# Constants of the last convolution chunk loaded ahead, and its last twelve frequencies multiplied on chip

## The chip, the cores and the metric

The kernel runs on one core of one Trainium2 chip. The metric is the device time of one execution in microseconds (us). The core has a matrix engine (TensorE, PE in the profile), a vector engine (VectorE, DVE), an engine for activation functions (ScalarE, ACT), a general one (GpSimd, POOL) and one that mainly issues transfers (SyncE, SP). Each has its own queue of instructions, and DMA transfers are issued from the queues of SP, ACT and POOL. Matmul results land in PSUM, which has eight banks; everything else on chip lives in SBUF. Between them and the memory outside (DRAM) only DMA moves data.

## The reference

The reference is a block with adaptive layer norm, a long convolution and a gated MLP, on 2048 positions of 640 channels, all in float32.

```python
mod = (_silu(c) @ w_mod).reshape(c.shape[0], 6, 1, -1)
sa, ca, ga, sb, cb, gb = (mod[:, 0], mod[:, 1], mod[:, 2], mod[:, 3], mod[:, 4], mod[:, 5])
h = _layernorm(x, axis=-1) * (1 + ca) + sa
x = x + ga * _A_ref(h, ...)     # y = causal convolution of h with K, over 2048 positions, plus h * Dskip
h = _layernorm(x, axis=-1) * (1 + cb) + sb
x = x + gb * _B_ref(h, B_w1, B_w3, B_w2)     # (silu(h w1) * (h w3)) w2, with 1728 inner columns
```

K is the real part of a sum of 128 complex exponentials for each channel. The reference applies it by FFT.

## The kernel before, in words

The kernel does the convolution by a Fourier transform written as matmuls. A position is a pair of 32 (`NA`) by 64 (`NB`), a frequency a pair of 32 `f` and 64. The 640 channels go in five **chunks** of 128 (`ch` 0 to 4), each chunk in eight **groups** (`g` 0 to 7) of four `f`. A group is numbered `k = 10 + 8 * ch + g`, so the last chunk has the numbers 42 to 49.

A group passes these stages. `stage2` (tile p of the trace) multiplies the transformed input and kernel, both in `uk`, by the constants `s2`, 256 KB a group. `k_copy` (kc) takes the kernel half out of PSUM on ACT. `products` (T and p) and `sums` (Y) form the complex products on DVE. `inverse1` (pz) multiplies them by the constants `i1`, again 256 KB a group. `z_store` copies the result to `zt` on ACT and stores it to the DRAM tensor `zs`. `s2` and `i1` are loaded anew for each group of each chunk, on SP's queue, into two buffers each, so that a load must wait for the group two before it.

The rest of the inverse transform sums over `f`: 16 tiles `j` of 128 positions read `zs` back with frequency on the partitions (`z_load`) and multiply it by `i2`. For the first four tiles that happens early: `x_part(j)` takes the first four chunks (tile py), adds `x` (xw, giving xm) and takes batch-norm statistics. Two places in PSUM, tagged pk and pb, hold py.

`ROUND` is an order written out by hand, run ten times. It makes the tables of the kernel K (phases `ph` on POOL, exponentials on ACT, products on DVE, `kgen` on PE) for later steps and runs the groups behind them. The loop over `tk` after it (line 981) finishes the groups of the last chunk. There the instructions are ordered by a planner with a cost model; `issue_after` puts an instruction behind another in a queue, and `keep_in_program_order` pins it.

The last chunk's end is written out in `z_last` (line 769). Each group is stored by itself, from ACT's queue. After group 5, POOL issues eight reads for `f` 0 to 23 of the four early tiles; after group 7, SP and ACT issue four each for `f` 24 to 31. `x_first` (line 1050) then runs ten matmuls on zeros that keep PE going, the 16 matmuls with `i2` on the last chunk (written to one bank `pl`, in the trace ps<-A,i), 18 more on zeros, and takes the second layer norm's statistics: three instructions for each tile on DVE, two small ones on POOL, one on DVE. The normalized rows (tile T) are transposed on PE, and the gated products begin (`plain`, then `seven` with fewer products, and `outputs`).

The first weights and the `x` tiles 4 and 5 are loaded on SP behind the last `i1` load (lines 1001 to 1009). `x_get` loads the `z` of the later tiles; the four places of `z_tile` are first held by the early tiles.

Phase tiles come from pool `tp` with three places (line 587), each 128 partitions by 32 x 67 words.

Of the kernel before, what the change touches and what calls it, by code (L numbers as in the profile page):

```python
# [33 lines left out]
NG = NA // 8  # L34
NPG = NPH + NG - 1
TURN = 4294967296.0
EPS = 1e-5


def consts():  # L40
# [6 lines left out]
    for q in range(4):  # L47
# [40 lines left out]
    f = lambda v: np.ascontiguousarray(v, dtype=np.float32)  # L88
    return {"s1": f(s1), "s2": f(s2), "i1": f(i1), "i2": f(i2), "iota": iota, "misc": f(misc),
            "ident": np.eye(P, dtype=np.float32)}  # L90
# [25 lines left out]
def tile_kernel(ctx: ExitStack, tc: tile.TileContext, a):  # L116
# [468 lines left out]
    def phases(s):  # L585
        sl = slice(s * SD, s * SD + 2 * SD)
        p = tp.tile([P, 2 * SD, NPG], I32, name="ph", bufs=3)
# [100 lines left out]
    def inverse1_load(g):  # L688
# [3 lines left out]
        return i1  # L692

    def stage2(ch, g):
        s2 = ahead.pop((ch, g, "s2"), None)
# [56 lines left out]

    zsv = zs.rearrange("k b c f d -> (c f) b k d")
    zsw = zs.rearrange("k b c f d -> k (b c) f d")

# [13 lines left out]
    def z_last(g):  # L769

        zt = fp.tile([P, 8, DC], F32, name="zt", bufs=2)[:, :4]
        acopy(zt.rearrange("p (i r) d -> p r i d", r=2), Zq[NDC - 1][:, :, (g % 2) * 2:(g % 2) * 2 + 2, :])
        S.dma_start(zsw[NDC - 1, :, g * 4:g * 4 + 4], zt)
        if g in (5, 7):
            fs = (0, 24) if g == 5 else (24, 32)
            for j in range(4):
                for c in range(2):
                    r = slice(c * 32 + fs[0], c * 32 + fs[1])
                    ins = (nc.gpsimd if g == 5 else S if c else nc.sync).dma_start(
                        early[j][1][64 + r.start:64 + r.stop, :, 2 * DC:], zsv[r, 4 * j:4 * j + 4, NDC - 1])  # L780
                    if g == 5 or c == 0:
                        zlast[g == 5] = ins


    def z_load(z, j, ks, q=nc.sync, b0=0):

        nb = z.shape[1]
        for k in ks:
            hh = int(k > 1)
            kk = k - 2 * hh  # L790
            q.dma_start(z[hh * 64:hh * 64 + 64, :, kk * DC:kk * DC + DC],
                        zsv[:, 4 * j + b0:4 * j + b0 + nb, k])

# [20 lines left out]

    early = []
    xe = []
# [146 lines left out]
    for rnd in range(NS // EB):  # L963
        if 2 <= rnd < 7:
            late_load(rnd - 2)
        for word in ROUND:
            name, k = word[:2].rstrip("+-"), EB * rnd + int(word[len(word[:2].rstrip("+-")):])
            if name in pieces:
                if 2 <= rnd < 7:
                    pieces[name](rnd - 2)  # L970
                continue
            do(name, k)
            if name == "E1" and 30 <= k < 38 and k % 2 == 0:
                x_load((k - 30) // 2)

            if name == "kg" and 36 <= k < 40:
                early.append((None, z_tile()))
                z_load(early[-1][1], k - 36, range(3), q=nc.gpsimd)
    in_order[0] = False

    for tk in range(NS + 1, LAG + 8 * NDC + 2):
        do("st", tk)
        do("kc", tk)
        last = do("iv", tk - 1)
        do("zt", tk - 1)
        do("T", tk)
        do("Y", tk)
        if tk == NS + 1:
# [4 lines left out]
            for j in range(4):  # L993
                early[j] = (x_tile(), early[j][1], xp.tile([P, KD, 6], F32, name="st5", bufs=4))
        i = tk - 1 - LAG - 8 * NDC + 8
        if 0 <= i < 8:
            if i < 4:
                z_load(early[i][1], i, (3,), q=nc.gpsimd)
# [31 lines left out]

    IDLE = (10, 18)

# [17 lines left out]
    def x_first(tiles):  # L1050

        keep_warm(IDLE[0])
        pl = bank(0).rearrange("p (i c) -> p i c", i=4)
        mv = xp.tile([P, 4, 2], F32, name="mv4", bufs=1)
        rs = xp.tile([P, 3, 4], F32, name="rs4", bufs=1)
        for j, (x, z, st) in enumerate(early):
            for b in range(4):
                c = slice(b * NA, b * NA + NA)
                tc.keep_in_program_order(PE.matmul(pl[c, j, :], i2[64:], z[64:, b, 2 * DC:], start=True, stop=True,
                                                   tile_position=(64, c.start)))  # L1060
        keep_warm(IDLE[1])
        for j, (x, z, st) in enumerate(early):
            V.tensor_tensor(x[:, 512:], pl[:, j, :], x[:, 512:], op=OP.add)
            V.bn_stats(st[:, 4, :], x[:, 512:])
            V.bn_aggr(mv[:, j, :], st)
        e = lambda i: epst[:, i:i + 1].broadcast_to([P, 4])
        G.tensor_tensor(rs[:, 0, :], mv[:, :, 1], e(0), op=OP.add)
        power = G.tensor_tensor(rs[:, 1, :], rs[:, 0, :], e(1), op=OP.pow)
        V.scalar_tensor_tensor(rs[:, 2, :], mv[:, :, 0], -1.0, rs[:, 1, :], op0=OP.mult, op1=OP.mult)
        for j, (x, z, st) in enumerate(early):  # L1070
# [5 lines left out]
            tiles.append(xn)  # L1076
        return power

# [380 lines left out]
    for pair in range(2):  # L1459
# [13 lines left out]
        if pair == 0:  # L1473
            tiles = []
            power = x_first(tiles)
            for k in range(KD):
# [120 lines left out]
```

## Time and profile before

| | us |
|---|---|
| median of 3 runs (lowest, highest) | 943.76 (942.69, 943.88) |
| the profiled execution | 944.3 |
| its span in the trace | 942.3 |
| PE busy | 874.9 |
| DVE busy | 699.1 |
| ACT busy | 541.6 |
| POOL busy | 268.4 |

The mean clock granted to PE is 0.963 of full speed. The profile shows one execution; the span runs from the first instruction to the last, and the execution's own time has 2.0 us more around it. All times in the text are us from the span's start.

In the trace, buffer numbers are left out of tile names, so `s` stands for `s2` and also for other tiles named s, and `i` for `i1` and `i2`. `L110` is a helper through which most instructions are recorded, so groups are told apart by their tiles. An entry in square brackets gives the time that an engine was idle just before an instruction and what ended it. A name like SPq or ACTq is an engine's queue, issuing a DMA.

### The profile page before, as it was taken

Reading aid. Unit: us, or ns where it says so; the run is one execution under the profiler, and the core shown is the slowest. Engines: PE = TensorE matmul, PEld = TensorE weight load, DVE = VectorE, ACT = ScalarE, POOL = GpSimd, SP = SyncE. Lnnn points to the kernel's source line nnn. Section 1 sums busy time; section 2 is a strip of 40 time slices with the busy share of each in tenths; the row PEclk is TensorE's granted clock in tenths of the full one; section 3 lists DMA queues with packets and bytes.
Section 4 is the critical chain, followed back from the end, with each engine's and each line's share of the span. In section 5 each row is a group of like instructions: output and inputs, shape, how many; then the busy total and the mean of one; then the engine's idle time right before and its main releaser. Section 6 shows DMA issues by size and latency. Waiting matters only on the chain.

```text
span 942.3 us, 19918 instructions
## 1 busy us (share of the span) xinstructions
PE 874.9 (93%) x7950; PEld 665.5 (71%) x7950; DVE 699.1 (74%) x1209; ACT 541.6 (57%) x747; POOL 268.4 (28%) x277
## 2 busy tenths in 40 slices
PE   3788989999988888999999999999999999999997
PEld 2445566666666655678888886678888888888885
DVE  5899899999999857686666655677876666664674
ACT  6989889999999432474333322465643333323332
POOL 3333544554444011223222201320332222200341
PEclk9777689999999999999999999999999999999999
DMA  9664476576666786952111227946312322123352
GB/s 273 208 221 177 150 204 211 175 214 192 180 201 179 206 254 201 274 191 85 56 57 56 56 71 204 268 143 197 117 51 57 112 56 57 56 85 97 102 199 77
DMA packets 103279, 140.66 MB, mean 149 GB/s; under 512 B 20276, under 2 KB 62388, under 8 KB 103188
## 3 DMA queue, kind: packets, MB, share of 16 engines
q1 hardware_dynamic: 92452, 113.45, 39.8%
q10 hardware_dynamic: 8432, 18.22, 6.4%
q0 software_dynamic: 2304, 7.74, 2.5%
q8 instruction: 62, 1.02, 0.5%
q14 instruction: 29, 0.24, 0.1%
HBM read 107.92 MB, written 31.46 MB: 148 GB/s over the span
## 4 chain that ended last, share of the span: by engine, by line
PE 66%; DVE 15%; ACT 6%; DMA 5%; SPq 4%; issue 3%; POOL 0%; DVEq 0%; ACTq 0%; POOLq 0%
PE ps L110 49%; PE p L110 6%; SPq L110 3%; PE pt L110 3%; PE pz L110 3%; DVE A L110 2%; PE pk L110 2%; DVE E L110 2%; DVE u L110 2%; PE pa L110 2%; DVE uk L110 1%; DMA s<-in_s_dram 1%; DVE st L110 1%; ACT cs L110 1%; ACT A L110 1%
## 5 line engine op out<-in xcount | busy, mean ns | idle before, releaser
L110 DVE TENSOR_TENSOR s<-ps,s 128x512 f32<-128x512 f32 x138 | 94.9, 688 | 83.0 <-PE ps L110 82.7
L110 ACT CAST gh<-rw 128x640 fp32r<-128x640 f32 x87 | 63.3, 728 | 130.0 <-PE ps L110 90.8
L110 DVE TENSOR_TENSOR gl<-rw,gh 128x640 fp32r<-128x640 f32 x87 | 77.3, 888 | 71.1 <-ACT gh L110 71.1
L110 POOL TENSOR_TENSOR S<-rw 128x256 f32<-128x256 f32 x46 | 36.6, 797 | 234.7 <-DVE S0l L110 158.1
L110 PE MATMUL p<-uk,s 128*64 128x256 f32 x640 | 80.9, 396 | 15.1 <-DVE Y L110 3.4
L110 PE MATMUL ps<-xA,gh 128*128 128x512 f32 x280 | 87.6, 391 | 0.4 <-ACT xA L110 0.4
L110 PE MATMUL ps<-gh,uh 128*128 128x512 f32 x224 | 87.8, 392 | 0.0
L110 PE MATMUL ps<-gl,uh 128*128 128x512 f32 x224 | 87.4, 390 | 0.0
L110 POOL TENSOR_TENSOR ph<-thi,iota 128x1376 int32<-128x1376 int32 x20 | 51.2, 2560 | 115.8 <-DVE A L110 94.6
L110 DVE TENSOR_TENSOR E<-A,cs 128x1024 f32<-128x1024 f32 (+1 forms) x80 | 81.0, 1024 | 2.5 <-PE pk L110 1.9
L110 PE MATMUL ps<-gh,ul 128*128 128x512 f32 x208 | 81.1, 390 | 0.0
L110 PEld LDWEIGHTS p<-uk,s 128*64 128x64 f32 x640 | 46.3, 140 | 39.3 <-DVE Y L110 5.7
L110 ACT ACTIVATE A<-pa 128x1024 f32<-128x1024 f32 (+1 forms) x80 | 64.2, 814 | 9.4 <-PE pa L110 8.9
L110 PEld LDWEIGHTS ps<-xA,gh 128*128 128x128 f32 x280 | 52.3, 188 | 12.9 <-issue 1.2
L110 DVE TENSOR_TENSOR A<-A,ph 128x1024 f32<-128x1024 f32 x40 | 54.2, 1358 | 0.8
L110 PE MATMUL ps<-xA,gl 128*128 128x512 f32 x140 | 54.5, 389 | 0.0
L110 PE MATMUL pt<-s,K 128*64 128x128 f32 x640 | 46.8, 291 | 5.4 <-ACT uk L110 5.4
L110 PE MATMUL pz<-Y,i 64*128 64x128 f32 x640 | 46.9, 286 | 2.4 <-DVE Y L110 1.6
L110 PEld LDWEIGHTS ps<-gh,uh 128*128 128x128 f32 x224 | 42.2, 188 | 9.4 <-DVE h L110 0.6
L110 PEld LDWEIGHTS pz<-Y,i 64*128 64x128 f32 x640 | 39.3, 188 | 13.3 <-issue 8.9
L110 PEld LDWEIGHTS ps<-gl,uh 128*128 128x128 f32 x224 | 42.2, 188 | 9.0
L110 PEld LDWEIGHTS pt<-s,K 128*64 128x64 f32 x640 | 37.1, 145 | 14.1 <-ACT uk L110 8.7
(214 smaller groups left out, 2156.5 us busy)
## 6 DMA issues: line engine op xcount, KB each, us to landing
rw<-in_w_dram ACTq DMA_DIRECT2D x44, 320.0 KB
us<-u SPq DMA_DIRECT2D x16, 640.0 KB
s<-in_s_dram SPq DMA_DIRECT2D x40, 256.0 KB
i<-in_i_dram SPq DMA_DIRECT2D x40, 256.0 KB
rw<-in_wg_dram SPq DMA_DIRECT2D x31, 320.0 KB
rw<-in_wu_dram SPq DMA_DIRECT2D x28, 320.0 KB
uk<-us SPq DMA_DIRECT2D x16, 512.0 KB
zs<-zt SPq DMA_DIRECT2D x16, 512.0 KB
```

Source lines behind the costliest of these rows:

```text
L110: ins = fn(*args, **kw)
```

## The change

It has two parts.

The first loads `s2` and `i1` of the groups 0 to 3 of the last chunk during the last two rounds, behind the `inverse1` of the groups 36 to 39. They go into two phase tiles that are used up by then. To outlive `tp`, phase tiles get a pool of their own.

The second ends the read-back at `f` 19 (`LATE = 5` groups). The last three groups, twelve frequencies, are multiplied straight from their `zt` tiles. For that the order of the partitions changes (in `i1` and `zs`), so that the positions of early tile `j` lie on the eight partitions from 32 `j` on, and a new constant `i2b` (three tiles, loaded on POOL in twelve DMAs) holds `i2` spread over four positions. The sums of all 32 frequencies then form in four banks, one for each early tile, and rows 20 to 31 that aren't read back are zero. `x_part` of tiles 2 and 3 moves to the place B. The statistics move from `x_first` to `x_stats`, ahead of the first weights' split, the first weights and `x` tiles queue behind the read-back, and the first ten matmuls on zeros go.

```diff
-    i1 = i1.reshape(P, NA // 2, 2, 2, NB).swapaxes(3, 4).reshape(P, NA // 2, 2, P)
+    i1 = i1.reshape(P, NA // 2, 2, 2, 4, 4, 4).transpose(0, 1, 2, 5, 4, 6, 3).reshape(P, NA // 2, 2, P)
+    f_late = np.arange(4 * LATE, NA)
+    i2late = np.stack([i2[f_late], i2[NA + f_late]])
+    i2b = np.einsum("lm,cfa->lcfma", np.eye(4), i2late).reshape(8, 8 - LATE, 4 * P)
...
-    zs = dram.tile([NDC, NB, 2, NA, DC], F32, name="zs")
+    zs = dram.tile([NDC, 4, 4, 4, 2, NA, DC], F32, name="zs")
...
+    php = ssm.enter_context(tc.tile_pool(name="php", bufs=3, side="right", reuse_waits="tile"))
+    def phase_tile():
+        return php.tile([P, 2 * SD, NPG], I32, name="ph")
...
+    def last_pair(g):
+        if g % 2 == 0:
+            kept.append(phase_tile().rearrange("p k b -> p (k b)").bitcast(F32))
+        for i, (name, src, n) in enumerate((("s2", a["s2"], 4), ("i1", a["i1"], 2))):
+            o = (g % 2 * 2 + i) * 4 * P
+            v = kept[-1][:, o:o + 4 * P]
+            v = v.rearrange("p (f c) -> p f c", f=4) if i == 0 else v.rearrange("p (f h c) -> p f h c", f=2, h=2)
+            nc.sync.dma_start(v, src[:, g * n:g * n + n])
+            ahead[NDC - 1, g, name] = v
...
-        S.dma_start(zsw[NDC - 1, :, g * 4:g * 4 + 4], zt)
-        if g in (5, 7):
-            fs = (0, 24) if g == 5 else (24, 32)
+        ztl[g] = zt
+        store = S.dma_start(zsw[NDC - 1, :, g * 4:g * 4 + 4], zt)
+        zlast[0] = store
+
+    def z_early():
+        with tc.issue_after(i1_last[0].ins):
             for j in range(4):
                 for c in range(2):
-                    r = slice(c * 32 + fs[0], c * 32 + fs[1])
-                    ins = (nc.gpsimd if g == 5 else S if c else nc.sync).dma_start(
-                        early[j][1][64 + r.start:64 + r.stop, :, 2 * DC:], zsv[r, 4 * j:4 * j + 4, NDC - 1])
+                    r = slice(c * 32, c * 32 + 4 * LATE)
+                    zlast[1] = nc.sync.dma_start(early[j][1][64 + r.start:64 + r.stop, :, 2 * DC:], zj(NDC - 1, j)[r])
+
+    def late_products(g):
+        zt, w = ztl[g], i2bt[g - LATE].rearrange("p (f c) -> p f c", f=4)
+        for f in range(4):
+            for j in range(4):
+                r = slice(j * 32, j * 32 + 8)
+                keep_order(PE.matmul(pls[j][:, :P], w[r, f, :], zt[r, f, :],
+                                     start=(g == LATE and f == 0), stop=(g == 7 and f == 3), skip_group_check=True,
+                                     tile_position=(j * 32, 0)))
+
+    def early_products():
+        for j, (x, z, st) in enumerate(early):
+            for b in range(4):
+                c = slice(b * NA, b * NA + NA)
+                keep_order(PE.matmul(pls[j][c, :P], i2[64:], z[64:, b, 2 * DC:],
+                                     start=False, stop=False, skip_group_check=True, tile_position=(64, c.start)))
...
+    def x_stats():
+        mv = xp.tile([P, 4, 2], F32, name="mv4", bufs=1)
+        rs = xp.tile([P, 3, 4], F32, name="rs4", bufs=1)
+        for j, (x, z, st) in enumerate(early):
+            V.tensor_tensor(x[:, 512:], pls[j][:, :P], x[:, 512:], op=OP.add)
...
-        py = [psS.tile([P, 512], F32, name="py", tag=t, bufs=1) for t in ("pk", "pb")]
+        if j < 2:
+            py = [psS.tile([P, 512], F32, name="py", tag=t, bufs=1) for t in ("pk", "pb")]
+        else:
+            if j == 2:
+                pys.append(psS.tile([P, 2, 512], F32, name="py", tag="B", bufs=1))
+            py = [pys[0][:, hh, (j - 2) * 256:] for hh in range(2)]
...
             do(name, k)
+            if name == "iv" and 36 <= k < 40:
+                with tc.issue_after(i1_last[0].ins):
+                    last_pair(k - 36)
...
     for tk in range(NS + 1, LAG + 8 * NDC + 2):
         do("st", tk)
         do("kc", tk)
+        if tk == LAG + 8 * NDC:
+            late_products(6)
         last = do("iv", tk - 1)
...
+                G.memset(early[j][1][64:, :, 2 * DC:], 0.0)
+            i2bt = [h_tile() for _ in range(8 - LATE)]
...
+            if i == 3:
+                with tc.issue_after(z_last_load.ins):
+                    for t in range(8 - LATE):
+                        for j in range(4):
+                            nc.gpsimd.dma_start(i2bt[t][j * 32:j * 32 + 8], a["i2b"][:, t])
             for j in ((), (), (), (), (0,), (1,), (), (2, 3))[i]:
                 x_part(j, last)
+            if i == 6:
+                pl = psS.tile([P, 2, 512], F32, name="pl", tag="A", bufs=1)
+                pls += [pl[:, 0], pl[:, 1]] + [psS.tile([P, 512], F32, name="pl", tag=t, bufs=1) for t in ("pk", "pb")]
+                late_products(5)
+            if i == 7:
+                z_early()
+                early_products()
+                late_products(7)
+    power = x_stats()
     for name in first_w:
         first_w[name] = xp.tile([P, KD, P], F32, name="rw", bufs=4)
-        with tc.issue_after(i1_last[0].ins):
+        with tc.issue_after(zlast[1].ins):
             w_get(first_w[name], 0, name)
...
     for i in range(2):
-        with tc.issue_after(i1_last[0].ins):
+        with tc.issue_after(zlast[1].ins):
             nc.sync.dma_start(x5[i], a["x"][(4 + i) * P:(5 + i) * P, :])
...
-    IDLE = (10, 18)
+    IDLE = 18
...
-        keep_warm(IDLE[0])
-        pl = bank(0).rearrange("p (i c) -> p i c", i=4)
...
+        keep_warm(IDLE)
+        mv, rs = moments
```

More of the change, by code (lines that the diff above doesn't have):

```diff
@@ L35 @@
 NPG = NPH + NG - 1
+LATE = 5
 TURN = 4294967296.0
@@ L692, in inverse1_load @@
         return i1
+    kept = []
+    def last_pair(g):
[7 more added lines that the diff above has]
+            ahead[NDC - 1, g, name] = v
     def stage2(ch, g):
@@ L751, in inverse1, with zj @@
         return ins
-    zsv = zs.rearrange("k b c f d -> (c f) b k d")
-    zsw = zs.rearrange("k b c f d -> k (b c) f d")
+    zsw = zs.rearrange("k q m l c f d -> k (q m l c) f d")
+    def zj(k, j):
+        return zs[k, j % 4, j // 4].rearrange("l c f d -> (c f) l d")
     def z_store(ch, g):
@@ new lines, in tile_kernel @@
+    keep_order = tc.keep_in_program_order
+    moments = []
+    def x_stats():
[3 more added lines that the diff above has]
+            V.tensor_tensor(x[:, 512:], pls[j][:, :P], x[:, 512:], op=OP.add)
+            V.bn_stats(st[:, 4, :], x[:, 512:])
+            V.bn_aggr(mv[:, j, :], st)
+        e = lambda i: epst[:, i:i + 1].broadcast_to([P, 4])
+        G.tensor_tensor(rs[:, 0, :], mv[:, :, 1], e(0), op=OP.add)
+        power = G.tensor_tensor(rs[:, 1, :], rs[:, 0, :], e(1), op=OP.pow)
+        V.scalar_tensor_tensor(rs[:, 2, :], mv[:, :, 0], -1.0, rs[:, 1, :], op0=OP.mult, op1=OP.mult)
+        moments.extend((mv, rs))
+        return power
@@ L790, in z_load @@
             kk = k - 2 * hh
-            q.dma_start(z[hh * 64:hh * 64 + 64, :, kk * DC:kk * DC + DC],
-                        zsv[:, 4 * j + b0:4 * j + b0 + nb, k])
+            ins = q.dma_start(z[hh * 64:hh * 64 + 64, :, kk * DC:kk * DC + DC], zj(k, j)[:, b0:b0 + nb])
+        return ins
     def x_tile():
@@ L813, in w_get @@
                 q.dma_start(w[i * 64:i * 64 + 64], a["w2"][f * P:f * P + 64, :])
-    early = []
+    early, pys = [], []
     xe = []
@@ L1050, in x_first @@
     def x_first(tiles):
-        keep_warm(IDLE[0])
-        pl = bank(0).rearrange("p (i c) -> p i c", i=4)
[L1054 to L1069, printed above, removed]
+        keep_warm(IDLE)
+        mv, rs = moments
         for j, (x, z, st) in enumerate(early):
@@ L1076, in x_first @@
             tiles.append(xn)
-        return power
     def x_get(j, x, loaded=False, homes=None):
@@ L1474, in tile_kernel @@
             tiles = []
-            power = x_first(tiles)
+            x_first(tiles)
             for k in range(KD):
```

9 lines of the change are left out of this document (4 added, 5 removed).

## The prediction

> **What bounds the kernel now.** I read the page first, then the windows, to find where TensorE (PE) stands still or runs at a lower clock, then the timelines of PE, SP and ACT there, and the chain of waits.
>
> ```profile
> PE 874.9 (93%) x7950; PEld 665.5 (71%) x7950; DVE 699.1 (74%) x1209; ACT 541.6 (57%) x747; POOL 268.4 (28%) x277
> 335.00:340.00 5.00, 2.69 (x28) 1.93 (x26) 2.14 (x4) 1.60 (x2) 0.00 (x0) 0.92 0.99 355
> 340.00:345.00 5.00, 5.00 (x42) 3.25 (x38) 2.14 (x4) 1.17 (x2) 2.44 (x4) 0.74 0.38 116
> 365.00:370.00 5.00, 3.00 (x49) 1.78 (x50) 3.31 (x13) 0.59 (x1) 3.46 (x6) 0.99 0.90 327
> 370.00:375.00 5.00, 4.94 (x34) 3.23 (x33) 2.00 (x5) 1.35 (x2) 1.19 (x3) 0.66 0.32 69
> ```
>
> A row of windows gives the stretch and its length, then busy us of PE, weight loads, DVE, ACT and POOL, then the granted clock, the DMA share and GB/s. PE is busy 93% of the span, so only stretches where it stands are worth much. Two lie together: 335 to 345, the start of the last chunk of the convolution, and 365 to 375, the seam to the gated products. In both, idle time is followed by a clock below 1 (0.74, 0.66).
>
> The first in detail: PE, the loads on SP, and the chain.
>
> ```profile
> 333.40 1.95 PE L110 MATMUL p<-uk,s 128*64 128x256 f32 x16
> 338.75 3.25 PE L110 MATMUL p<-uk,s 128*64 128x256 f32 x16 [2.31 <-DMA s<-in_s_dram]
> 341.93 1.48 PE L110 MATMUL pz<-Y,i 64*128 64x128 f32 x16
> 343.35 1.95 PE L110 MATMUL p<-uk,s 128*64 128x256 f32 x16
> 345.22 1.16 PE L110 MATMUL pz<-Y,i 64*128 64x128 f32 x16
> 349.12 1.16 PE L110 MATMUL pz<-Y,i 64*128 64x128 f32 x16 [0.85 <-DMA i<-in_i_dram]
> 350.77 1.52 PE L110 MATMUL p<-uk,s 128*64 128x256 f32 x12 [0.49 <-DMA s<-in_s_dram]
> 332.02 6.59 DMA s<-in_s_dram
> 345.33 5.39 DMA s<-in_s_dram
> ```
>
> The p rows are stage2 of groups 0 (333.40), 1, 2 and 4, the pz rows inverse1. An s2 load starts only when the group two earlier has left its place, and takes 6.59 and 5.39 us; PE catches up with it twice. Lost: 2.31 + 0.85 + 0.49 idle, and at the low clock 3.25 - 1.95 = 1.30 and 1.48 - 1.16 = 0.32. Together **5.27 us**.
>
> The second, from group 6's inverse1 on:
>
> ```profile
> 362.74 1.16 PE L110 MATMUL pz<-Y,i 64*128 64x128 f32 x16
> 365.45 1.22 PE L110 MATMUL pz<-Y,i 64*128 64x128 f32 x16 [1.55 <-DVE Y L110]
> 366.61 0.66 PE L110 MATMUL py<-A,i 64*32 64x256 f32 x16
> 367.84 0.99 PE L110 MATMUL py<-A,i 64*32 64x256 f32 x16 [0.57 <-DVE xm L110]
> 369.81 4.11 PE L110 MATMUL ps<-idle 128*128 128x512 f32 x10 [0.98 <-DVE xm L110]
> 373.85 1.32 PE L110 MATMUL ps<-A,i 64*32 64x128 f32 x24
> 375.36 0.42 PE L110 MATMUL ps<-A,i 64*32 64x128 f32 x8 [0.20 <-DMA A<-zs]
> 375.71 4.40 PE L110 MATMUL ps<-idle 128*128 128x512 f32 x18
> 375.84 0.49 DVE xm L110 x2
> 379.76 1.74 ACT T L110 x2
> 357.44 0.33 ACTq L110 DMA_DIRECT2D zs<-zt  x1
> 364.56 0.33 ACTq L110 DMA_DIRECT2D zs<-zt  x1
> 367.34 0.33 ACTq L110 DMA_DIRECT2D zs<-zt  x1
> 366.54 4.64 POOL L779 DMA_DIRECT2D A<-zs  x8 [21.64 <-DMA xm<-in_x_dram]
> 369.88 1.77 ACTq L110 DMA_DIRECT2D A<-zs  x4
> ```
>
> Group 7 is stored at 367.34 and read back from 369.88; only then come the last products (ps<-A,i), done at 375.36 + 0.42 = 375.78. Statistics follow at once (375.84), the power on POOL, then normalized rows (379.76). So from 363.90, where group 6's pz ends, 11.9 us pass to 375.78, of which 4.11 are matmuls that only keep PE going.
>
> **The change part by part.**
>
> *Preload.* s2 and i1 of groups 0 to 3 come during the two rounds before. The buffers of fp then hold groups 4 and 5 already from about 332. Groups 6 and 7 still load two groups ahead, but before they showed no idle time. What is late next? PE itself: 345.22 - 343.35 = 1.87 for a p and about 1.09 for a pz make 2.96 a group, which the rows from 343.35 on already keep. Gain **5.27**.
>
> *Its price.* Eight loads of 256 KB, 2 MB, move on SP's queue to behind the i1 loads of the rounds.
>
> ```profile
> 300.31 0.33 SPq L691 DMA_DIRECT2D i<-in_i_dram  x1
> 316.81 0.33 SPq L691 DMA_DIRECT2D i<-in_i_dram  x1
> 321.22 0.58 SPq L685 DMA_DIRECT2D s<-in_s_dram  x1
> 329.56 1.95 PE L110 MATMUL p<-uk,s 128*64 128x256 f32 x16
> 310.00:315.00 5.00, 3.44 (x48) 2.88 (x46) 4.49 (x10) 3.27 (x4) 1.83 (x3) 1.00 0.98 257
> 325.00:330.00 5.00, 5.00 (x112) 3.75 (x110) 2.75 (x7) 1.08 (x3) 0.00 (x0) 1.00 0.33 89
> ```
>
> The four pairs land between the i1 loads of 300.31 and 316.81 and the few us behind them. The DMA share there is up to 0.98, so they queue: a pair is 512 KB, 2.0 us at 257 GB/s. Behind them wait the s2, i1, u loads and z stores on SP. The load of 321.22 is used at 329.56, 8.3 us later; at 6.59 us to land it has 1.7 us to spare. Bounds: 0 (DVE, busy 4.49 of 5, sets the pace) to 4.0 (the time of two pairs, unhidden). I take **+0.5**, near the first, since PE's own waits in these rows are not for DMA. Their places are free: phases 34 and 36 are used up in the round before.
>
> The Trainium skill, DMA: Bandwidth & Descriptors (Issuing engines are not separate DMA queues) says all engines' DMAs share the same 16 DMA engines and interleave; by it the 2 MB are paid in full wherever the share is 1, some 2 us more. No row here shows the pairs yet.
>
> *Late products.* Sixteen fp32 matmuls a group, recorded as 32 instructions of 128 columns on four row groups of 8 rows, three times. The trace has none like it. Nearest rows: pz, two row groups, same columns: 16 in 1.09 from start to next start (so 8 steps of 0.136 side by side), and pa, 32 rows:
>
> ```profile
> 62.38 0.66 PE L110 MATMUL pa<-r,lx 32*128 32x512 f32 x4
> 304.12 0.50 PE L110 MATMUL pa<-r,lx 32*128 32x512 f32 x2
> L110 PEld LDWEIGHTS pz<-Y,i 64*128 64x128 f32 x640 | 39.3, 188 | 13.3 <-issue 8.9
> ```
>
> Four row groups take 0.66 where two take 0.50, so four do run together. Below: 1.09 a group (8 steps). Between: 2.18, if two at a time. Above: single file, 32 x 0.136 = 4.36. I take 1.2, nearest to the pa rows. The Trainium skill, TensorEngine Tiling (Key Properties) speaks against it: changing the tiling mode drains the engine, and the change adds some four switches. Here p, pz and py alternate modes and start 1.87, 1.09 and 0.6 apart without visible gaps, so its price is small.
>
> *The seam's sum.* From 363.90: late products of 5 and 6 (2.4, covering the 1.55 idle), pz 1.2, py 0.66, the wait on the shared banks of B 0.57, py 0.66, early products 1.1 (32 instructions at 1.32/24 = 0.055 are 1.76 at the low clock, about 1.1 at 1.0), late product of 7 1.2: 7.8, so 371.7 instead of 375.78. **Gain 4.1.** The sum holds if the clock stays near 1: idle here falls from 3.1 us to under 1.
>
> Covers. The read-back on SP (eight issues of about 0.33, 2.6 us) needs group 4's store only. A store issued at 367.34 was readable by 369.88, 2.5 us; so 357.44 + 0.33 + 2.5 = 360.3, issues until 363, landed by about 366, needed at 369.4. Without that cover each us late is a us lost. That it waits for group 4 alone rests on a row: the store of 364.56 went out before the POOL reads of 366.54, so rows of other frequencies are kept apart. First weights and x tiles 4, 5 queue behind these reads; landing about 369 to 371, their casts are needed only behind the transposes. POOL loses eight issues (4.64) and gains twelve small ones, at 4.64/8 = 0.58 about 7 us, and four memsets; its row shows 21.64 us of idle time before 366.54, and group 5's four land by 352. ACT loses 1.77.
>
> Added waits: the 18 warm matmuls now need a bank that holds the sums until DVE has read them (0.5 to 1.6 us), then take 4.40, against 4.0 from 375.78 to 379.76 and 1.74 for the rows; behind them on PE stand the transposes. 0 to 0.8; I take +0.3. DVE's two weight remainders may fall into POOL's wait, 0 to 1.6; I take **+0.2**.
>
> ```profile
> 374.33 3.27 SPq L110 DMA_DIRECT2D A<-zs  x5
> 392.00:396.00 4.00, 4.00 (x35) 2.98 (x41) 3.33 (x7) 0.81 (x2) 0.74 (x3) 1.00 1.17 208
> ```
>
> *Behind the seam* DMA is full (1.17). Its first z loads (374.33) wait for places that the last products free and for group 7's store: both come about 4 us earlier, so I let the stage move along whole.
>
> Sum: -5.3 + 0.5 - 4.1 + 0.3 + 0.2 = **-8.4 us**. The profiled execution took 944.3 (span 942.3 and 2.0 around it): 935.9. That execution stood 0.5 above the median of 943.76, so the forecast is 935.4.
>
> **The rivals.**
>
> *Late products two at a time* (2.18): 3 x 0.98 = 2.9 more, 938.3. For: pz shows two row groups, none shows 128 columns on four. Against: pa.
>
> *The preload is paid in the rounds*: 2.0 for each of two pairs that find the queue full, 3.5 more than I took: 938.9. For: 0.98. Against: 0.33 at 325 to 330. It is what the skill's rule on shared DMA engines would give.
>
> *The seam gains nothing*: reads wait for group 7's store after all, land near 375, products end as before: -5.3 + 0.5 gives 939.0. Against: the stores' row above.
>
> *The change doesn't do what it says*: the planner puts the preloads where their places are not yet free, so SP's queue stands and the s2 stalls stay: only the seam is left, 3.6 us: 940.2.
>
> *Slower*: late products in single file with weight loads uncovered. A weight load of 128 columns lasts 188 ns in the page's pz group. 96 instructions at p us cost 96p instead of 3.6; the gain of 8.4 is gone at p = 0.125. At 0.188 they cost 18.0: 14.4 more, 949.8. For: the trace has no matmul of 8 rows by 128 columns, so nothing shows its weight loads covered. Against: pz's 16 in 1.09, 68 ns each, with weight loads of the same width. In single file with covered loads (0.136) the time is 944.9, no change.
>
> *The clock*: with the ten warm matmuls gone, the seam's end may run like them (4.11 for 10, at 0.66 to 0.71): 18 take 7.4 instead of 4.4, 3 more, 938.4. It is in the range.
>
> **How the numbers follow.** Forecast 0.68; two at a time 0.10; rounds 0.08; seam nothing 0.05; not as said 0.03; slower 0.06. The range, 932 to 940.5, takes in the forecast's bounds (3 us below, if loads behind the seam gain too) and the rivals up to 939. A measurement tells 0.2% (1.9 us) from no change: faster 0.89, same 0.04, slower 0.07.
>
> **What would show it.** No idle before p by s loads between 333 and 351, clock 1.0 there, group 4's p near 345.4; no new DMA waits of PE between 300 and 333. Three runs of 32 matmuls of about 1.1 us each; last products some 8 us after group 6's pz; the normalized rows (T) about 9 us earlier than 379.76. Wrong if late products last over 2 us each, if PE waits for A<-zs, or if the z loads behind start no earlier.

## The result, and the profile after

The changed kernel takes **936.1 us** (median of six runs, 935.3 to 939.53), the kernel before beside it on the same chip 944.11 (six runs, 942.69 to 948.65): a ratio of 0.9911, with a 95% interval of 0.9889 to 0.9933. The forecast was 935.4, with a range of 932.0 to 940.5.

The profiled execution of the changed kernel is the slowest of its six, 939.53 us, with a span of 937.6: 3.4 us above the median. The text says below where it lost time. First the page's row of engines, then rows of its windows (columns as before). In this kernel the recording helper is line 114.

```profile
PE 875.5 (93%) x8036; PEld 668.3 (71%) x8036; DVE 700.2 (75%) x1209; ACT 541.3 (58%) x747; POOL 272.7 (29%) x285
```

```profile
320.00:325.00 5.00, 3.94 (x146) 2.86 (x146) 4.20 (x8) 2.09 (x3) 0.00 (x0) 1.00 1.05 371
335.00:340.00 5.00, 5.00 (x66) 3.69 (x64) 2.77 (x5) 2.66 (x8) 0.53 (x1) 1.00 0.92 297
340.00:345.00 5.00, 5.00 (x56) 3.32 (x54) 3.66 (x8) 2.34 (x4) 0.00 (x0) 1.00 0.70 256
365.00:370.00 5.00, 3.04 (x96) 2.12 (x80) 4.07 (x18) 0.44 (x1) 0.00 (x0) 0.99 0.97 319
370.00:375.00 5.00, 4.30 (x10) 3.46 (x11) 3.36 (x12) 1.68 (x3) 2.24 (x3) 0.50 0.98 214
```

PE now works through all of 335 to 345, at clock 1.00. The second stretch, 365 to 375, still holds idle time, and its clock has fallen from 0.66 to 0.50. And in 320 to 325, where the last preloads pass, the DMA share is 1.05. So the first hole is closed, the second only in part. The timeline of PE in the changed kernel, cut to the ends of the stages, shows both:

```profile
315.91 1.95 PE L114 MATMUL p<-uk,s 128*64 128x256 f32 x16 [1.57 <-issue]
...
322.07 1.95 PE L114 MATMUL p<-uk,s 128*64 128x256 f32 x16 [1.06 <-DMA s<-in_s_dram]
...
336.71 1.95 PE L114 MATMUL p<-uk,ph 128*64 128x256 f32 x16
...
348.59 1.95 PE L114 MATMUL p<-uk,s 128*64 128x256 f32 x16
...
358.68 1.95 PE L114 MATMUL p<-uk,s 128*64 128x256 f32 x16
...
361.65 2.07 PE L114 MATMUL pl<-zt,h 8*128 8x128 f32 x64
363.65 1.16 PE L114 MATMUL pz<-Y,i 64*128 64x128 f32 x16
...
366.32 0.67 PE L114 MATMUL py<-A,i 64*32 64x256 f32 x16 [0.92 <-DVE xm L114]
366.78 1.08 PE L114 MATMUL pl<-A,i 64*32 64x128 f32 x32
367.79 1.17 PE L114 MATMUL pl<-zt,h 8*128 8x128 f32 x32
370.70 7.19 PE L114 MATMUL ps<-idle 128*128 128x512 f32 x18 [1.73 <-DVE xm L114]
377.72 2.35 PE L114 MATMUL ps<-ident,T 128*128 128x128 f32 x20
379.82 0.48 PE L114 MATMUL ps<-xA,gh 128*128 128x512 f32 x1
```

Group 0 of the last chunk starts its stage2 at 336.71, from a phase tile (p<-uk,ph), group 4 at 348.59, group 7 at 358.68. The late products are the rows pl<-zt,h; the first 64 belong to groups 5 and 6. The last of them ends at 367.79 + 1.17 = 368.96. Behind them PE stands 1.73 us, then 18 matmuls on zeros take 7.19 us at half clock.

To add up the difference, four rows of the kernel before that were not shown yet, from the timelines of PE and DVE: group 38's and group 7's stage2, the first gated product, and the ninth writing of a tile h on DVE. The second fence has the last of these for the changed kernel.

```profile
313.73 1.95 PE L110 MATMUL p<-uk,s 128*64 128x256 f32 x16 [1.56 <-issue]
...
360.86 1.95 PE L110 MATMUL p<-uk,s 128*64 128x256 f32 x16
...
383.16 0.48 PE L110 MATMUL ps<-xA,gh 128*128 128x512 f32 x1
...
451.71 0.68 DVE L110 TENSOR_TENSOR h<-s,s 128x512 f32<-128x512 f32 x1
```

```profile
446.65 0.68 DVE L114 TENSOR_TENSOR h<-s,s 128x512 f32<-128x512 f32 x1
```

| point (us from the start) | before | changed | difference | its step |
|---|---|---|---|---|
| stage2 of group 38 | 313.73 | 315.91 | +2.18 | +2.18 |
| stage2 of group 0, last chunk | 333.40 | 336.71 | +3.31 | +1.13 |
| stage2 of group 7 | 360.86 | 358.68 | -2.18 | -5.49 |
| end of the last products | 375.78 | 368.96 | -6.82 | -4.64 |
| normalized rows (T) | 379.76 | 374.67 | -5.09 | +1.73 |
| first gated product | 383.16 | 379.82 | -3.34 | +1.75 |
| ninth h | 451.71 | 446.65 | -5.06 | -1.72 |
| end of the span | 942.3 | 937.6 | -4.7 | +0.4 |

The first step, 2.18 us, is there before the first pair of preloads is issued at 302.91: a stage2 that starts at 302.13 in the kernel before starts at 304.31 here. Stage2 of group 38 stands at 313.6 to 316.5 in the twelve experiments, at 313.58 in another execution of the unaltered changed kernel (e11_changed_again) and at 315.91 here. So the step belongs to the execution. Without it the profiled pair would differ by 6.9 us.

### The profile page after: what moved, and what is told of

Its sections match the earlier page's. It is cut to its first block, busy times and chain, and to the rows that moved or that the text cites. A ratio compares the mean times of both kernels' runs of the same rounds, so it can differ in the third digit from the quotient of the medians.

```text
span 937.6 us, 20100 instructions
## 1 busy us (share of the span) xinstructions
PE 875.5 (93%) x8036; PEld 668.3 (71%) x8036; DVE 700.2 (75%) x1209; ACT 541.3 (58%) x747; POOL 272.7 (29%) x285
## 4 chain that ended last, share of the span: by engine, by line
PE 74%; ACT 9%; DVE 8%; issue 3%; SPq 3%; DMA 3%; DVEq 0%; ACTq 0%
PE ps L114 54%; PE p L114 7%; PE pz L114 4%; PE pt L114 3%; SPq L114 3%; PE pk L114 2%; PE pa L114 2%; ACT A L114 2%; ACT cs L114 1%; DVE uk L114 1%; DVE u L114 1%; ACT ph L114 1%; PE pu L114 1%; ACT uk L114 1%; ACT L114 1%
## 5 line engine op out<-in xcount | busy, mean ns | idle before, releaser
L114 PE MATMUL p<-uk,s 128*64 128x256 f32 x576 | 71.6, 391 | 15.2 <-DVE Y L114 3.9
L114 PEld LDWEIGHTS p<-uk,s 128*64 128x64 f32 x576 | 41.3, 138 | 36.9 <-DVE Y L114 5.6
L114 ACT ACTIVATE s<-ps 128x512 f32<-128x512 f32 (+1 forms) x33 | 19.7, 597 | 45.8 <-PE ps L114 45.8
L114 POOL TENSOR_TENSOR rw<-rw,gbr 128x512 f32<-128x512 f32 x14 | 20.4, 1458 | 88.7 <-DMA rw<-in_w_dram 77.3
```

Of the source, the lines that this page charges most:

```text
L114: ins = fn(*args, **kw)
```

## The experiments

Twelve runs follow; one of them is the changed kernel once more. The diffs are against the changed kernel, except those of e1 (against the kernel before) and e12 (against e8). Ratios are against the kernel before on the same chip (its medians there were 944.6 to 945.0), with the 95% interval in brackets. "xA" is the first gated product, as in the table.

### The two parts alone

First the preloads without the rest: the kernel before with phase tiles in their own pool, `last_pair` and these lines.

```diff
             do(name, k)
+            if name == "iv" and 36 <= k < 40:
+                with tc.issue_after(i1_last[0].ins):
+                    last_pair(k - 36)
```

> The kernel before with the first part alone: phase tiles in a pool of their own, s2 and i1 of groups 0 to 3 loaded in the rounds; the seam as before. Theory (the two parts add): the waits for s2 and i1 at the start of the last chunk go (5.3 to 5.5 us) and about 1.1 us come back at the second but last group of the rounds, where an s2 load now lands late: net -4 to -4.5 us, ratio 0.9955. Rival (what the preload saves is given back in the rounds or behind the seam): within 1 us of before. In the trace: no idle time of PE for s or i loads in the last chunk, one of about 1 us in the rounds.

Measured: 939.28 us (937.36 to 942.24), ratio 0.994 [0.9923, 0.9957], so about 5.7 us less than before. Then the rest without the preloads; these three lines are taken out of the changed kernel.

> The changed kernel without the preload; the late products, the new statistics and the phase pool stay. Theory: from group 6's inverse1 to the last products 7.2 us instead of 11.9, of which the later statistics (weight remainders between them) and the warm matmuls at half clock give back 1 to 3: net -2 to -4 us, ratio 0.996 to 0.998. Rival (the seam gives nothing, all of the gain is the preload): within 0.5 us of before. The waits for s2 of 2.3, 0.85 and 0.5 us stay in the trace.

Measured: 942.15 us (938.25 to 944.13), ratio 0.9971 [0.9954, 0.9987], about 2.7 us less. The two parts add up to 8.4, and the whole measures 8.4 (0.0089 x 944), so no interaction is seen. One of 2 us could hide, though: each of the three figures has an interval of 1.6 to 2.1 us to either side, and the whole measured again (e11, below) gives 6.5. PE's timeline with the preloads alone:

```profile
320.77 1.95 PE L110 MATMUL p<-uk,s 128*64 128x256 f32 x16 [1.13 <-DMA s<-in_s_dram]
...
335.42 1.95 PE L110 MATMUL p<-uk,ph 128*64 128x256 f32 x16
...
357.39 1.95 PE L110 MATMUL p<-uk,s 128*64 128x256 f32 x16
```

From group 0 to group 7 it takes 357.39 - 335.42 = 21.97 us, the same as the changed kernel's 358.68 - 336.71 = 21.97; before, 360.86 - 333.40 = 27.46. The preload is worth 5.49 us there, and it pays 1.13 in the round, so 4.4 are left, as expected. The measured 5.7 is more; in the trace, e1 gains another 1.1 behind the seam (67.5 us from xA to the ninth h, where the kernel before takes 68.5). With the seam alone, a stall appears on DVE that the prediction had only as a possibility. DVE's timeline:

```profile
378.04 0.83 DVE L114 TENSOR_TENSOR gl<-rw,gh 128x640 fp32r<-128x640 f32 x1 [2.88 <-DMA A<-zs]
378.78 0.28 DVE L114 BATCH_NORM_AGGREGATE mv<-st 128x2 f32<-128x30 f32 x1
```

The remainder of the first weights (gl) stands ahead of the last mean and variance (mv), and waits 2.88 us for what SP's queue brings behind the read-back; the statistics wait with it. Without the preloads that transfer comes later still.

### The late products in single file

The same 96 instructions, but with the four row groups taken one behind the other, so that neighbours use the same eight rows.

```diff
-        for f in range(4):
-            for j in range(4):
+        for j in range(4):
+            for f in range(4):
```

> The changed kernel with the late products in another order: all four frequencies of one early tile before the next tile, so that neighbours in the queue use the same eight rows. Same instructions, same result. Theory (row groups run side by side in the changed kernel): each run of 32 takes up to 32 x 0.136 = 4.4 us instead of 1.0, three of them about 10 us more in the seam; less where PE waited anyway; total +7 to +10 us over the changed kernel, about as slow as before or slower. Rival (PE takes them out of order or the pace is set by something else): within 1 us of the changed kernel.

Measured: 944.37 us (939.68 to 946.48), ratio 0.9981 [0.996, 1.0003]: what is left of the gain, 0.2%, can't be told from none. Single file costs 0.0070 in ratio, 6.6 us, a little less than the 7 to 10 expected. PE's timeline, then its windows:

```profile
362.27 5.38 PE L114 MATMUL pl<-zt,h 8*128 8x128 f32 x64
...
374.37 5.13 PE L114 MATMUL pl<-zt,h 8*128 8x128 f32 x32
```

```profile
365.00:370.00 5.00, 5.00 (x55) 4.37 (x61) 0.00 (x0) 0.28 (x1) 0.00 (x0) 0.68 0.81 256
370.00:375.00 5.00, 4.08 (x67) 2.57 (x52) 3.07 (x12) 0.30 (x1) 0.00 (x0) 0.50 0.20 73
```

The first 64 take 5.38 us, 84 ns each (the last 0.8 us of them at half clock), where the changed kernel has 2.07, 32 ns each: side by side is 2.6 times as fast as recorded, some 2.4 times at equal clock. That settles the rivals "two at a time" and "single file". It also shows something new: PE is busy for all of 365 to 370, and still the clock falls, to 0.50 from about 366.9 to 384. The last 32 then take 5.13.

### What holds the seam's end

Three edits, each for one of the waits behind the last products. The first runs eight matmuls on zeros in place of 18.

```diff
-    IDLE = 18
+    IDLE = 8
```

> The changed kernel with 8 warm matmuls instead of 18 in front of the transposes. Theory (warm matmuls that start late, after the sums have been read, and run at half clock hold the transposes back by about 1.5 us): 8 of them end before the normalized rows are ready, so the transposes start with the rows: -1 to -1.5 us against the changed kernel, where its clock was low. Rival (they are needed; without them the clock is lower behind the seam): the first products run at half clock for up to 3.4 us, +1 to +2 us.

Measured: 938.42 us (937.3 to 940.35), ratio 0.9925 [0.9903, 0.9947]; no gain. The eight take 3.75 us, the transposes start with the rows, at 374.34, but take 4.14 in place of 2.35, since the clock is low for 10 us.

The second orders the first weights' remainder behind the last mv.

```diff
+    stats_end = [None]
...
-            V.bn_aggr(mv[:, j, :], st)
+            stats_end[0] = V.bn_aggr(mv[:, j, :], st)
...
-        ws = plain_weights(simple[0], last_sum if pair == 0 else None)
+        ws = plain_weights(simple[0], stats_end if pair == 0 else None)
```

> The changed kernel, with the remainders of the first weights (gl, ul) put behind the last statistics instruction (mv) on DVE; before, the planner set gl in front of it, and gl waits for the first weights, which now queue behind the read-back. Theory (statistics wait for a weight transfer): the last mv ends 1.2 us earlier, right behind the others, and the normalized rows start about 1 us earlier; -0.5 to -1.2 us against the changed kernel (ratio to before 0.990). Rival (the rows wait for the warm matmuls and transposes anyway): rows earlier, transposes not, time as the changed kernel.

Measured: 937.49 us (935.22 to 939.22), ratio 0.9921 [0.9901, 0.9942]. The rows T come 14.89 us behind group 7's stage2, not 15.99, but the transposes start only at 376.82, behind 18 matmuls on zeros that took 6.98. The statistics weren't what PE waited for.

The third puts the 18 into the PSUM place Z, which is free, directly behind the late products, instead of into a bank that DVE must first have read.

```diff
+    warm = psS.tile([P, 2, 512], F32, name="pz", tag="Z", bufs=1)[:, 0]
+    for _ in range(18):
+        keep_order(PE.matmul(warm, idle[:, :P], idle, start=True, stop=True))
     power = x_stats()
...
-        keep_warm(IDLE)
```

> The changed kernel, with the 18 warm matmuls written to a PSUM place that is free earlier (Z) instead of one that is held until DVE has read all sums. Theory (the idle 1.7 us in front of them, on top of 0.9 before, is what lets the clock fall to half): they start right behind the late product of group 7, run at 0.24 us each, end before the normalized rows are ready, and the transposes start with the rows: -1.5 to -2 us against runs of the changed kernel with the low clock, 0 against the others; ratio to before 0.989 to 0.991. Rival (the late products of 8 rows themselves let the clock fall): they start early and still run at 0.4 us each.

Measured: 939.67 us (936.55 to 941.78), ratio 0.9939 [0.9918, 0.996]. The wait is gone, the transposes start with the rows, and xA comes 3.18 us behind T in place of 5.15. PE's timeline:

```profile
367.91 5.98 PE L114 MATMUL pz<-idle 128*128 128x512 f32 x18
```

But the 18 take 5.98, not 4.4: the clock fell to 0.50 for 3.4 us though nothing stood idle in front of them. So the idle 1.7 us isn't what lets it fall, at least not alone. The rival, that the late products themselves let it fall, isn't shown either: in e8, e10 and e12 the same late products stand in front, and the clock holds. And the kernel is no faster: from xA to the ninth h it takes 69.4 us, where the changed kernel takes 66.8.

### The price in the rounds

The pairs are loaded later, behind the groups 37, 39, 40 and 41.

```diff
-            if name == "iv" and 36 <= k < 40:
+            if name == "iv" and k in (37, 39, 40, 41):
                 with tc.issue_after(i1_last[0].ins):
-                    last_pair(k - 36)
+                    last_pair((37, 39, 40, 41).index(k))
```

> The changed kernel, with the four pairs of preloads issued behind the inverse1 of groups 37, 39, 40 and 41 instead of 36 to 39. Theory (the 1.1 us of PE's wait for s2 in the rounds, with a landing of 9.7 us, comes from the pairs ahead of that load in a full queue): the wait is gone or under 0.3 us, the preloads still come in time, -0.8 to -1.1 us against the changed kernel. Rival (the wait only moves to the next loads): a wait of about 1 us elsewhere between 320 and 345, time unchanged.

Measured: 937.02 us (934.0 to 938.71), ratio 0.9913 [0.9893, 0.9934]. The wait for s in the round is gone: from group 38 to group 0 it takes 19.79 us (313.67 to 333.46), as before (19.67). In the ratio, the 1.1 us can't be told from nothing. The three later runs with the pairs in these places take 20.32 (e8, still with a wait of 0.58 for s), 19.96 (e10) and 19.67 (e12).

Then this edit with the two before it (statistics first, 18 in Z):

> The three edits of the runs before this one together. Theory (they lie behind one another on the path): the sum of their gains, -2 to -4 us against the changed kernel, 932 to 934 us, ratio to before 0.987 to 0.989. Rival (only one of them was on the path): no more than the best of the three.

Measured: 936.92 us (935.26 to 939.33), ratio 0.9917 [0.9898, 0.9936]. The seam does what was hoped: the clock stays at 1.00, the 18 take 4.38, xA comes at 374.58, 5.2 us ahead of the changed kernel's, of which 2.2 are the earlier front (313.72). But from xA to the ninth h it takes 69.8 us, 3.0 more.

### Where the gain behind the seam goes

Two theories: the loads behind the seam can't start earlier, or the instructions stand in another order. For the first, the weights and `x` tiles 4 and 5 are loaded ahead of the read-back, alone and with the three edits.

```diff
+            if i == 4:
+                for name in first_w:
+                    first_w[name] = xp.tile([P, KD, P], F32, name="rw", bufs=4)
+                    with tc.issue_after(i1_last[0].ins):
+                        w_get(first_w[name], 0, name)
...
-    for name in first_w:
-        first_w[name] = xp.tile([P, KD, P], F32, name="rw", bufs=4)
-        with tc.issue_after(zlast[1].ins):
-            w_get(first_w[name], 0, name)
```

> The changed kernel, with the first weights and the x tiles 4 and 5 (1.3 MB) loaded on SP during groups 4 and 5 of the last chunk, where the DMA share is 0.56 to 0.7, instead of behind the read-back, where it is 1. Theory (behind the seam the z loads of the tiles 4 to 7 set the pace in a full DMA, so that work saved on PE there is given back): the z loads finish up to 3 us earlier and the first products with them, -1 to -3 us against the changed kernel; also no wait of the statistics for weights. Rival (PE, ACT or DVE set the pace behind the seam): z loads earlier, time as the changed kernel. A loss is possible if s2 of group 6 comes late behind these loads: a wait of 1 to 3 us before its p.

> The edit of the run before together with the three earlier ones (statistics ahead of the weight remainders, warm matmuls in an early place, pairs later). Theory (DMA behind the seam hid the gains of the three): now they show, -3 to -5 us against the changed kernel, ratio to before 0.986 to 0.988. Rival: no better than each alone, 0.990 to 0.992.

Measured: 936.43 us (933.91 to 937.7), ratio 0.9911 [0.9893, 0.993], and with all four edits 937.9 (936.84 to 941.65), ratio 0.9939 [0.9917, 0.996], again with 69.8 us from xA to the ninth h. The unaltered changed kernel ran beside them:

> The changed kernel again, beside the two others on the same chip. All theories: ratio to before 0.990 to 0.993; the wait for s2 of about 1 us in the rounds and the warm matmuls behind an idle 1.7 us come back; the front part before 310 us may lie up to 2.5 us earlier or later than in the first profile, as that part is the same code in all runs.

Measured: 938.6 us (935.54 to 939.91), ratio 0.9931 [0.9912, 0.995]. So loading the first weights earlier didn't recover the three us. It also costs: from group 0 to group 7, e9 takes 23.3 us and e10 23.4, where the changed kernel takes 22.0, as ACT's copy of group 2's result waits there for an earlier store and PE for ACT. For the second theory the instructions from xA on were compared in the built kernels. The kernels of the runs e2, e3, e5, e7 and e9 have the changed kernel's order on PE, DVE and ACT, and take 66.8 to 67.0 us to the ninth h, with xA anywhere from 375.55 to 388.11; e11, the changed kernel itself, takes 67.4. In the kernel before, 15 places on DVE and 5 on ACT differ, and it takes 68.5; in those of e6 and e8, 33 and 35 places on DVE, 14 and 15 on ACT and 42 and 46 on PE. By their traces, e1 has the order of the kernel before on PE, DVE and ACT, and takes 67.5, and e4 has another order on DVE and ACT, and takes 68.8. The last run restores the changed kernel's order: the three edits, but with eight matmuls in Z and the 18 in their old bank besides.

```diff
-    for _ in range(18):
+    for _ in range(8):
         keep_order(PE.matmul(warm, idle[:, :P], idle, start=True, stop=True))
...
+        keep_warm(IDLE)
```

> As the kernel with all three edits (pairs after the groups 37, 39, 40, 41; first weights' remainder behind the statistics), but only eight matmuls on zeros stand in place Z behind the late products, and the 18 stand again in their old bank behind the statistics. With these 18 the instructions of PE, DVE and ACT from the first xA on stand in the same order as in the changed kernel; without them (18 in Z alone) 46 places of PE, 35 of DVE and 15 of ACT differed. Theory that the order behind the seam gave back the gain: from the first product of xA to the ninth h again 66.8 us (not 69.8), transposes with the rows as before, xA 36 to 38 us behind group 7's p less 20 (about 16 to 17 behind it), ninth h near 442, time about 2 to 3 us under the changed kernel's in the same conditions, ratio about 0.989. Rival (what is given back comes from transfers, or from any seam that ends earlier, whatever the order): 69 us or more to the ninth h, ratio as before, about 0.992. Second rival (the 18 in the old bank bring the low clock back): they take 6 us or more, transposes late, no gain over the changed kernel.

Measured: 937.82 us (933.23 to 940.38), ratio 0.9919 [0.9891, 0.9948]. PE's timeline of this kernel:

```profile
366.16 2.10 PE L114 MATMUL pz<-idle 128*128 128x512 f32 x8
368.33 4.42 PE L114 MATMUL ps<-idle 128*128 128x512 f32 x18
...
373.48 2.18 PE L114 MATMUL ps<-ident,T 128*128 128x128 f32 x18 [0.18 <-ACT T L114]
375.41 0.48 PE L114 MATMUL ps<-xA,gh 128*128 128x512 f32 x1
...
402.26 1.20 PE L114 MATMUL ps<-ident,T 128*128 128x128 f32 x9 [1.71 <-ACT T L114]
```

The 18 take 4.42, so the clock holds, and the transposes wait only 0.18 for the rows. The ninth h comes at 444.22, 68.8 us behind xA: neither 66.8 nor 69.8. PE now stands 1.71 at 402.26, where the changed kernel's PE runs through. The chain of waits says on what; its columns are the start, the duration and the piece of work.

```profile
375.72 5.24 DMA A<-zs
...
381.64 8.04 DMA T<-in_x_dram
...
390.16 4.62 DMA rw<-in_wu_dram
...
395.67 2.23 POOL rs L114 x6
...
402.26 0.78 PE ps L114 x5
```

In this kernel the chain runs through loads for the next tiles and of weights, then statistics on POOL and rows on ACT. In the changed kernel's chain it is PE alone there; but in e11, the same kernel in another execution, the chain leaves PE halfway for a load of weights, and then takes the same way as in e12. First the changed kernel, then e11:

```profile
381.04 24.49 PE ps L114 x142
```

```profile
377.06 11.52 PE ps L114 x67
...
388.58 5.26 DMA rw<-in_wu_dram
```

With the order of e8, the chain goes through DVE instead, and PE waits there for a weights' remainder:

```profile
396.92 0.57 DVE T L114
...
399.11 0.70 DVE gl L114
...
399.85 3.71 PE ps L114 x17
```

So neither theory holds alone. Counted from group 7's stage2, xA comes at 21.1 us in the changed kernel, and at 20.0 and 19.9 in e7 and e9, which still take 66.8 and 67.0 to the ninth h. At 19.6 (e11) it is 67.4, with the chain through loads. So, as far as one profile of each can tell, little more than 1 us can be won at the seam's end before the loads take the rest. In e12 xA comes hardly earlier, at 19.5, yet it takes 68.8, since its loads are late themselves: SP issues the weights in its chain 34.2 us behind group 7's stage2, those of e11 32.4 us behind. Why they are later isn't shown. The kernels with another order (e6, e8, e10) take 2.6 to 3.0 more than the changed kernel, and their chains go through DVE or ACT; restoring the order won back only 1.0. None of the twelve runs is faster than the changed kernel beyond its interval.

## Why the prediction held, step by step

**Preload, 5.27.** Measured 5.49, twice, with the same rows. No wait for s or i is left in the last chunk, the clock is 1.00, and the groups stand 2.97 apart. PE itself was next, as said. Group 4 came at 348.59, not 345.4: 2.2 of that is the late front of this execution, 1.1 the price.

**Its price, 0.5.** Measured 1.1 in this execution and in e1. In all eight executions with the pairs in these places, from group 38 to group 0 it takes 0.7 (e9) to 2.2 us (e6) more than before, so the price changes with the execution. The sign "no new DMA waits of PE between 300 and 333" failed. The spare time was read from one load, issued at 321.22 with 1.7 us to spare; the one that came late is another, for an earlier p. The chain of the changed kernel has it:

```profile
312.31 9.71 DMA s<-in_s_dram
...
322.07 1.95 PE p L114 x16
```

It takes 9.71 us to land, not 6.59, since the pairs are in front of it and the DMA share is 1.05. With the pairs behind other groups the wait is gone in e7, e10 and e12, and 0.58 in e8. The sentence of the Trainium skill on shared DMA engines, DMA: Bandwidth & Descriptors (Issuing engines are not separate DMA queues), had the direction right: the share is above 1 and a load is late. The rival built on it, two pairs at 2 us each, isn't seen: PE waits once, 1.06 us here and 2.11 in the worst execution (e6).

**Late products, 1.2 each.** Measured 2.07 for two and 1.17 for the third, so 3.24 against 3.6. The pa rows were the right neighbours. The Trainium skill's note on changing the tiling mode, TensorEngine Tiling (Array Packing) (Key Properties), isn't contradicted, but no gap shows: the 64 start at 361.65 and the next pz 2.00 behind.

**The seam, 4.1.** From the end of group 6's pz, which is 361.72, to the last product 368.96 - 361.72 = 7.24, where 7.8 were forecast and 11.88 stood before: 4.64. The read-back was in time; no early product waits for it. SP's timeline:

```profile
359.60 3.43 SPq L807 DMA_DIRECT2D A<-zs  x8
...
367.24 4.04 SPq L114 DMA_DIRECT2D A<-zs  x5
```

The eight issues begin at 359.60 (forecast 360.3). The z loads of the next tiles begin at 367.24, 7.1 us earlier than before, where "about 4" was said.

**Added waits, 0.3 and 0.2.** This is the term that was mis-sized: 1.73 + 1.75 = 3.5 us in the profiled execution. In e11 it is 2.0, so the term was too small there too. Half of it stands between the last product and the rows T, which were forecast some 9 us earlier than before and come 5.1 earlier (7.3 without the late front). Timelines of DVE and ACT of the changed kernel:

```profile
371.57 0.83 DVE L114 TENSOR_TENSOR gl<-rw,gh 128x640 fp32r<-128x640 f32 x1 [0.44 <-DMA A<-zs]
372.31 0.28 DVE L114 BATCH_NORM_AGGREGATE mv<-st 128x2 f32<-128x30 f32 x1
...
374.67 1.74 ACT L114 ACTIVATE T<-xm,rs 128x640 f32<-128x640 f32 x2 [2.51 <-DVE rs L114]
```

The remainder gl was costed in POOL's wait behind the statistics; the planner put it ahead of the last mv, where it waits for its weights, 0.44, and runs 0.83. The other half is the clock. The rows are there at 374.67 + 1.74 = 376.41, the transposes start at 377.72: the 18 matmuls on zeros started late and ran slowly, the rival that was written down for 938.4. It happened in this execution. In e11 the same 18 took 5.67, and xA came 3.8 behind T in place of 5.15, against 3.40 before. That the ten missing matmuls on zeros cause it, as the rival has it, isn't shown: e1 still has the ten, and its 18 take 5.98. The profiled execution is 3.1 us longer than e11's; 2.3 of that are its late front, 1.3 the slower way from T to xA, of which 0.6 come back behind it.

**Behind the seam, "moves along whole".** It gained 1.7 more (66.8 us from xA to the ninth h against 68.5). The forecast named the cause, loads behind the seam, in the bound 3 us below it, but not in the sum. The chain of the kernel before runs there through loads that are issued late:

```profile
385.84 6.72 DMA A<-zs
...
394.77 6.75 DMA rw<-in_wg_dram
```

In the changed kernel the first z loads are issued 12.6 us ahead of xA, before 8.8, and its chain is PE alone. The order of instructions differs too, but it can't be all of it: e1 has the order of before, z loads 10.0 us ahead of xA, and takes 67.5. So of the 1.7, 1.1 came without the new order; whether the rest is the order or still earlier loads is open.

So two gains were forecast a little too small (by 0.2 and 0.5), one wasn't in the sum (1.7), and two costs were too small (by 0.6, and by 3.0 in the profiled execution, 1.5 in e11). That the total came out at 8.4 is in part luck, since these cancel: the mechanisms of both parts are as forecast, but not every term. The slower rival needed single file, and e3 shows that single file loses nearly all of the gain, 6.6 us.

## What to carry to other kernels

A stall that the trace shows row by row (idle before an instruction, and what ended it, plus the low clock behind it) can here be priced to half a microsecond. Waits that the change adds are where the error lies, so look at what the planner places between the new instructions, and at whether the bank in PSUM that the next one writes is still being read. When an end is brought forward, ask how far the next limit is: here the gain of further edits vanished after little more than 1 us, at loads or behind an order of instructions that the planner had changed with the edit. And since one execution of the same kernel differed by 4 us from another, differences between two profiles should be taken stage by stage from a common point.

## What the runs showed of the hardware

**A clock that comes in steps of time.** At the seam the granted clock was 0.50 for about 3.4 us (the kernel before, e1, e2, e6, e7, e9, e11), 6.8 us (e5 and the profiled changed kernel), 10 us (e4), 17 us (e3), and not at all in e8, e10 and e12. The Trainium skill, TensorE: Matmul & The Clock Gate (What's actually happening), has a free-running window of some 3.4 us, with the clock halved after an idle window and restored after a busy one. These lengths, all near a multiple of it, agree with the window; that the halving takes an idle one doesn't agree with e3 (below). The same kernel had 6.8 in one execution and 3.4 in another. What made the clock fall at this seam stays open: it fell with the ten matmuls on zeros (e1) and without, and with idle time before the 18 (e11) and without (e6).

**Busy is not enough.** In e3 the clock fell while PE was recorded as busy for 5.00 of 5.00 us (365 to 370), with matmuls of 8 rows up to 367.65. It stayed at 0.50 from 366.8 to 370.2, where PE was again busy throughout. The profile doesn't show what the throttle counts; the busy share doesn't tell it.

**Four row groups of eight rows run side by side.** Taken in turn, an instruction of 128 columns takes 32 ns (changed kernel, 64 in 2.07 us); with neighbours on one row group it takes 84 ns (e3, 64 in 5.38 us, the last 0.8 us at half clock).
